# One set of state transfers for two batches, and a new instruction order, in a fused mLSTM and gated feed-forward kernel

## The chip, the cores and the metric

The kernel runs on one core of a Trainium2 chip. The metric is the device time of one execution in microseconds (us), as the median of several runs; less is better.

## The reference

The first half is an mLSTM with exponential gates over four batches, eight heads, 768 steps and a head width D of 40. The second half is a gated feed-forward network over the 3072 rows that come out of it.

```python
for t in range(S):                                   # S = 768
    m_new = np.maximum(f_gate[:, :, t] + m, i_gate[:, :, t])
    f_stab = np.exp(f_gate[:, :, t] + m - m_new)
    i_stab = np.exp(i_gate[:, :, t] - m_new)
    C = f_stab * C + i_stab * (v_t outer k_t)        # state, D x D for each head
    n = f_stab * n + i_stab * k_t
    y[:, :, t] = sigmoid(o_t) * (C q_t) / max(|n q_t|, 1)
x = y as (batch * step, head * D)                    # 3072 x 320
out = (sigmoid(x @ w_gate) * (x @ w_val)) @ w_out    # inner width 1536
```

## The kernel before

The steps are cut into six chunks of 128, so there are 24 units of work (chunk c, batch b), numbered u = 4c + b. Within a chunk the mLSTM is computed as masked attention: scores of q and k (`b` steps, line 778 for the first eight units and 783 from unit 8 on), times a decay matrix, times v (`c` steps, line 761). What the earlier chunks left behind enters through the state: the `ci` step (line 804) multiplies q by the state of its batch, and the `c` steps of chunks 1 to 4 also form the outer products of k and v that update the state (line 629).

The state lives in two forms. The tile `cst` holds the state of each head, two heads above each other, and is updated in place by VectorE, GpSimd or ScalarE (`z`, `zm` for chunk 0, `zd` and `za` later). The tile `cb` is a block-diagonal copy that `ci` reads as its right operand, three heads to a block. Since a block moves data to other partitions, it is filled by transfers: the `zs` steps, four for each unit of chunks 0 to 4, which the table `MOVES` lists (`moved`, line 923). That is 80 transfers.

From unit 8 on q and k are turned by a detour through memory: a step `a` transposes in blocks, `as` steps save pieces to the scratch tensors `scr0q`, `scr0k`, `scr1q`, `scr1k` (line 713, even and odd batches), `s` steps load them again as `qs` and `ks` (line 748), and `aq` steps load `qk` for `ci` (line 720). `ks` and `qs` have one buffer each, so the loads of a unit start when the scores of the unit before it are done.

The feed-forward half is 103 tiles of TensorE work: `t` steps are the up products (line 951, output 256 or 512 columns wide), `p` steps the down products (line 989). All large operands are held as a high and a low part. In the opening the weights are decoded by ScalarE and VectorE from loads named `st`.

Nearly all transfers are issued from one queue, SyncE's (SP), in program order. Each waits until the eighth transfer before it has landed. The order of all instructions on all engines is written out by hand in the string `ORDER`: a word is the next step of that name. An engine takes its instructions strictly in that order.

Of the kernel before, what the change touches and what calls it, by code (L numbers as in the profile page):

```python
# [9 lines left out]
F32 = mybir.dt.float32  # L10
# [132 lines left out]
p9*2 p10 t11 p9 t12 cf5 t12 p9 t12*2 w20f t12 tg11 p10 p9 gs w21e zs2 t12 w23d w25a k1d w25b w24a lo8 t12 e6 t12*2
w25b p10 t12 / b5.2 gs*2 k1d w23f p10 w24b t12 bm5.2 k1d t12*3 th11 tl11 al8.0 w24b p10*2 cx4 w24b w24d w23e / a6.2
t12 lo7 zd5 as8.3 ta12 p10 w24e p10 t12 w26a ah6.2 d4 w27a dx4 zs2 c5 cs5 cv5 dy4 t13 cv5 tg12 p11 t13*3 p11 w25b w24f
e6m lq7 t13 w26b t13 a6.1 w26b p11 ah6.1 lv9 t13 w27b w26b za5 th12 t13*3 p11 ct5 p11 cg5 t13 p11 cv5 w25d t13 w25e
p11*2 p12 w26d p12 p11 lk7 t13 lv6 / ci6 tl12 t13 w26e cr5 p11 w27b t13 as8.1 p12*2 e7a p12 w27b p12*2 ta13 lq9 t13
p12 t14*6 tg13 cf6 t14*3 cx5 aq6.0 d5 t14 a7.2 lo6 w27d p11 ld8 as8.0 a9.1 t14*2 zs4*2 w27e t14 p11 bk6 ah7.2 / b6.0
t14*2 aq6.2 p12 t14 as8.2 dx5 dy5 p12 zs4 aq6.1 th13 bm6.0 p13 b6.1 ct7 w27f w28a b6.2 tl13 aq7.2 bm6.1 zd7 bm6.2 e7m
ta14 w28b p13*2 t15*2 zd6 tg14 t15 a7.1 w28b lq11 ah7.1 w28b c6 t15*3 p12 t15 e8 a7.0 w28d p12 aq7.1 t15 za6 w28e ld9  # L150
th14 t15*2 p13 tl14 p13 w29a t15*2 ah7.0 t15 p13 lv8 t15*2 ct6 lk8 w29b p13 lv7 cs6 w29b ah9.1 cv6 ta15 zs5 p13 t15
w29b cg6 / ci7 w29d p13*2 p14 al9.1 cv6 tg15 t16 p13 t16 cf7 t16 p13 t16 aq8 t16 zs4 t16 th15 p14 zs6 as9.7 p14 t16*2
as9.5 bk7 / b7.1 w29e p14 as9.4 t16 aq8 t16 lq12 t16 p15 bm7.1 a8.1 p15 t16 p14 tl15 t16 p14*2 ah8.1 al8.1 t16 as8.4
p15 oh0 a9.0 t16 as9.6 cv6 / b7.2 ta16 t16 tg16 p15 p14 p15 p14 t17*2 as8.6 t17*3 o0 t17 as8.7 p14 t17 p14 p15*2 cr6
p15 bm7.2 aq7.0 b7.0 t17*2 ah9.0 th16 aq8 t17 p14 t17 tl16 p15 bm7.0 t17*4 ta17 p15 c7 cs7 oh1 p16 zs5 t17 tg17 al9.0
p15*2 t18 cx6 d6 t18 th17 p16 as8.5 t18*2 e8a t18*4 tl17 t18*2 ld10 a11.0 p16 dx6 dy6 p16 v8 t18 p17 o1 t18*5 p17 p16
as9.0 e8m p17 s8 p16 ta18 s8 p17 t19*2 cv7 tg18 cg7 t19*3 s8 t19*2 e9a oh3 th18 t19 p18 s8 bk8 a10.0 zs5 p17*2 t19*5
cv7 tl18 t19*2 / ci8 cf8 ct8 ta19 t19 p18 tg19 p18*2 t20*4 th19 as9.2 t20*4 / b8.2 ah10.0 o3 tl19 t20 bm8.2 cv7 v9
al10.0 t20*6 ta20 t20 p19 cr7 tg20 p19 oh2 lk10 p19 p18 th20 p18 lq14 as9.1 t21*2 p19 t21*6 tl20 za7 t21*2 e10a t21*2
p20 t21*3 ta21 cx7 / b8.1 b8.0 bm8.1 t21 p19 t22*2 tg21 t22*6 lo10 th21 a10.1 p20*2 p21 bm8.0 p19 zs7 p20 t22*2 lo9  # L160
p21 t22*2 p20 as9.3 t22*4 d7 e9 tl21 c8 ta22 tg22 t23*2 zs6*2 t23 ah10.1 as10.0 ah11.0 t23 p20 t23 zd8 cs8 cv8 s9*2
t23*4 al10.1 t23*2 th22 t23*2 as10.2 t23 p21 t23 aq9 p22*2 t23 dx7 tl22 p21*2 ta23 p22 tg23 p21 t24 th23 e9m bk9 t24
cv8 dy7 cv8 aq9 t24*2 p22 t24*5 as10.5 al11.0 zs6 p22 p23 t24 as10.6 t24*2 p22 t24 zs7 zs5 t24*2 cg8 p23 tl23 aq9 ci9
t24 ta24 s9 p23 t25*2 tg24 s9 as10.3 t25 lv11 t25*5 th24 p23 t25*3 v11 t25 za8 t25*3 p23 t25 p23 p24*2 tl24 as10.1 p24
ta25 t26*2 p24 as10.4 cf9 tg25 t26*2 ct10 t26*6 v10 t26*3 p24 t26 cr8 th25 t26 p24 tl25 lv10 t26 / b9.1 ta26 b9.0 t27
tg26 p25*2 bm9.1 p25*2 as10.7 t27*6 zs7 t27*4 zd10 t27*2 th26 t27*3 p25 p26 tl26 p26 b9.2 ta27 tg27 t28*3 o2 lk11
# [91 lines left out]
t102*4 p100*6 p101*2 o20 p101 ta102 tg102 th102 p101*2 p102*2 tl102 p102 oh22 o22 p101 p102*3 oh23 o23  # L258
"""
GROUPS = ((0, 3), (3, 3), (6, 2))  # L260
PAIRS = ((0, 3, 6, 2), (1, 4, 7, 5))
MOVES = ((0, 0, 0, 0, 3), (1, 1, 0, 0, 3), (2, 0, 3, 0, 1), (2, 1, 3, 1, 2))


@with_exitstack
def mlstm_then_gated_ffn_kernel(
# [13 lines left out]
    nc = tc.nc  # L280
    B, H, S, D = q.shape
    P = 128
# [926 lines left out]
```

## Time and profile before

| what | us |
|---|---|
| median of 3 runs | 518.26 (517.64 to 519.38) |
| the profiled execution, its own time | 519.33 |
| its span, first to last instruction | 517.6 |
| TensorE (PE) busy in the span | 501.0 (97%) |
| VectorE (DVE) / ScalarE (ACT) / GpSimd (POOL) busy | 311.6 / 190.5 / 154.5 |
| bytes moved by DMA | 76.67 MB in 234782 packets |

The profiled execution is 1.7 us longer than its span, and 1.07 us longer than the median of the runs. The granted TensorE clock is full over the whole span up to the last output. In the views, SPq means SP's queue: a row there is a transfer being issued. Such a row shows its issue, not its data.

### The profile page before, as it was taken

To read this page: it belongs to the slowest core of one execution; us is meant where nothing else is said; L and a number is where in the kernel's file an instruction comes from. 1 tells how busy PE (TensorE), PEld (TensorE's weight loads), DVE (VectorE), ACT (ScalarE), POOL (GpSimd) and SP (SyncE) were. 2 spreads that over 40 slices of the span, in tenths; PEclk is the share of its full clock that TensorE was granted. 3 is DMA by queue.
4 is the path that set the end of the run, shared out by engine and by line. 5 is a ranking of instruction groups with operands and counts; after the bars stand their busy time and mean duration, and the time that the engine had idled before them with its cause. 6 is when DMAs were issued, how large, how long until landed. Compare 5 with 4: busy or idle time off the path is not lost.

```text
span 517.6 us, 13246 instructions
## 1 busy us (share of the span) xinstructions
PE 501.0 (97%) x5191; PEld 453.0 (88%) x5191; DVE 311.6 (60%) x738; ACT 190.5 (37%) x483; POOL 154.5 (30%) x207
## 2 busy tenths in 40 slices
PE   7899999999998999999999999999999999999997
PEld 6678887889898999998887888888888888999997
DVE  8898989886653675655656464786544234434222
ACT  5876675653333324324213133211331441222221
POOL 3654342445352222331212242403241320101011
PEclk9999999999999999999999999999999999999999
DMA  8988886867968888996788689798699752010001
GB/s 194 209 220 215 231 229 170 180 149 141 201 128 172 171 184 174 183 206 109 154 169 141 152 172 201 142 175 170 151 166 215 135 115 77 26 27 15 13 1 39
DMA packets 234782, 76.67 MB, mean 148 GB/s; under 512 B 214240, under 2 KB 222624, under 8 KB 234720
## 3 DMA queue, kind: packets, MB, share of 16 engines
q1 hardware_dynamic: 233632, 75.56, 68.1%
q8 instruction: 41, 0.67, 0.5%
q10 hardware_dynamic: 1088, 0.26, 0.3%
q14 instruction: 21, 0.17, 0.1%
HBM read 57.61 MB, written 17.14 MB: 144 GB/s over the span
## 4 chain that ended last, share of the span: by engine, by line
PE 71%; DMA 9%; DVE 7%; SPq 6%; ACT 3%; issue 3%; POOL 1%; ACTq 0%; DVEq 0%
PE pg L951 42%; PE po L989 20%; PE av L761 2%; SPq L923 2%; PE s L783 2%; DMA st<-in_moe_w_val_dram 2%; PE in L804 2%; DMA qs<-scr1q 2%; DMA st<-in_moe_w_gate_dram 1%; DMA qs<-scr0q 1%; SPq L713 1%; DMA out_dram<-ob 1%; PE xt L888 1%; SPq L748 1%; DVE dc L535 1%
## 5 line engine op out<-in xcount | busy, mean ns | idle before, releaser
L964 ACT ACTIVATE sg<-pg 128x256 f32<-128x256 f32 (+1 forms) x103 | 48.3, 469 | 238.1 <-PE pg L951 211.1
L967 DVE SCALAR_TENSOR_TENSOR sg<-sg,pg 128x256 f32<-128x256 f32 (+1 forms) x103 | 54.0, 524 | 114.9 <-ACT sg L964 88.8
L978 POOL TENSOR_TENSOR gl<-sg,gh 128x256 fp32r<-128x256 f32 (+1 forms) x51 | 50.1, 982 | 233.6 <-ACT gh L972 82.9
L951 PE MATMUL pg<-xh,wh 128*128 128x256 f32 (+1 forms) x412 | 110.1, 338 | 0.6 <-ACT sg L964 0.5
L951 PE MATMUL pg<-xl,wh 128*128 128x256 f32 (+1 forms) x412 | 109.2, 329 | 0.5 <-DVE xl L901 0.4
L951 PE MATMUL pg<-xh,wl 128*128 128x256 f32 (+1 forms) x412 | 107.7, 331 | 0.0
L989 PE MATMUL po<-ol,gh 128*128 128x320 f32 x288 | 87.4, 314 | 0.0
L989 PE MATMUL po<-oh,gh 128*128 128x320 f32 x288 | 87.1, 315 | 0.3 <-ACT ob L1005 0.3
L989 PE MATMUL po<-oh,gl 128*128 128x320 f32 x288 | 85.7, 312 | 0.0
L951 PEld LDWEIGHTS pg<-xl,wh 128*128 128x128 f32 x412 | 69.8, 188 | 5.7 <-DVE xl L901 0.9
L951 PEld LDWEIGHTS pg<-xh,wh 128*128 128x128 f32 x412 | 69.1, 189 | 6.5 <-ACT sg L964 1.0
L951 PEld LDWEIGHTS pg<-xh,wl 128*128 128x128 f32 x412 | 68.9, 188 | 5.6
L951 PE MATMUL pg<-xl,w 128*128 128x256 f32 (+1 forms) x206 | 61.9, 334 | 0.0
L989 PEld LDWEIGHTS po<-oh,gh 128*128 128x128 f32 x288 | 53.2, 188 | 4.6 <-ACT ob L1005 0.7
L989 PEld LDWEIGHTS po<-ol,gh 128*128 128x128 f32 x288 | 53.4, 188 | 3.6
L989 PEld LDWEIGHTS po<-oh,gl 128*128 128x128 f32 x288 | 53.4, 188 | 3.5 <-DVE gl L978 0.2
L951 PE MATMUL pg<-xh,w 128*128 128x256 f32 (+1 forms) x206 | 55.0, 330 | 0.0
L789 DVE TENSOR_TENSOR d<-s,d 128x384 f32<-128x384 f32 (+1 forms) x66 | 32.8, 507 | 29.5 <-PE s L783 26.9
L972 ACT ACTIVATE gh<-sg 128x256 fp32r<-128x256 f32 (+1 forms) x58 | 28.9, 498 | 40.2 <-DVE sg L967 27.3
L481 ACT ACTIVATE d<-d,at 128x128 f32<-128x128 f32 x136 | 42.9, 390 | 0.0
L951 PEld LDWEIGHTS pg<-xl,w 128*128 128x128 f32 x206 | 36.7, 188 | 2.2
L951 PEld LDWEIGHTS pg<-xh,w 128*128 128x128 f32 x206 | 34.8, 188 | 2.5
(151 smaller groups left out, 671.6 us busy)
## 6 DMA issues: line engine op xcount, KB each, us to landing
d<-mscr SPq DMA_DIRECT2D x22, 512.0 KB
k<-in_k_dram SPq DMA_DIRECT2D x24, 160.0 KB
v<-in_v_dram SPq DMA_DIRECT2D x24, 160.0 KB
o<-in_o_gate_dram SPq DMA_DIRECT2D x24, 160.0 KB
st_o<-in_moe_w_out_dram SPq DMA_DIRECT2D x12, 320.0 KB
scr0q<-qt SPq DMA_DIRECT2D x32, 120.0 KB
out_dram<-ob SPq DMA_DIRECT2D x24, 160.0 KB
scr1q<-qt SPq DMA_DIRECT2D x32, 120.0 KB
```

What stands on the lines that cost most here:

```text
L481: nc.scalar.activation(d[:, h, :], d[:, h, :], AF.Exp, bias=at[:, c, b * H + h : b * H + h + 1], scale=-1.0)
L761: nc.tensor.matmul(dst[xs], lhs[:, xs], rhs, start=True, stop=True)
L783: nc.tensor.matmul(ps[g][:, m, :], ks[: 3 * D, h0 + m, :], qs[: 3 * D, h0 + m, :], start=True, stop=True)
L789: nc.vector.tensor_tensor(x, ps[g][:, :nh, :], x, ALU.mult)
L804: nc.tensor.matmul(pi[:, h0 : h0 + nh, :], qk[u][:r, g, :], cb[:r, b, g, : nh * DA], start=True, stop=True)
L923: nc.sync.dma_start(cb[j * D : (j + 1) * D, b, g0:g1, j * DA : (j + 1) * DA], pair_state(b)[88 * e : 88 * e + D, p0 : p0 + g1 - g0, :])
L951: nc.tensor.matmul(pg[x], w[:, a, fs] if a < 2 else w[:, fs], y[c][:, a, n0:n1], start=first, stop=a == 2 and y is xl)
L964: nc.scalar.activation(sg[0], pg[0], AF.Tanh, scale=0.5)
L967: nc.vector.scalar_tensor_tensor(sg[0], sg[0], 1.0, pg[1], ALU.add, ALU.mult)
L972: nc.scalar.activation(gh[u][:, :nt], sg[0], AF.Copy)
L978: E('gl0' if c == 0 else 'gl', f'tl{n}').tensor_tensor(gl[u][:, :nt], sg[0], gh[u][:, :nt].bitcast(F32), ALU.subtract)
L989: nc.tensor.matmul(po[t], g[c, j, t0][:, (t - t0) * P : (t - t0 + 1) * P], o[:, j, :], start=j == 0 and first, stop=j == NF - 1 and last)
```

## The change

The tiles `cst` and `cb` are laid out anew, so that the two batches of a pair (0 and 1, 2 and 3) stand beside each other. A `zs` step now moves the part of both batches, and only the odd batch of a pair has such steps: 40 transfers in place of 80, each with twice the rows. A row stays 41 numbers long, 164 bytes. A set now waits for the states of both batches, and, since it overwrites what `ci` reads, for the `ci` of both. `GAP` is 0, so the scratch tensors and their loads stay as they were.

`ORDER` differs from its 21st word on, in the opening too. Its words are the same but for the 40 that go.

```diff
-v1 lk1 lq1 iy ig v0 ig im ia ir is ig im ih igs iac ih x2
+v1 lk1 lq1 iy ig ir x2 ig ...
...
-    cb = const.tile([P, B, 3, 3 * DA], F32, name="cb")
+    cb = const.tile([P, B // 2, 3, 2, 3 * DA], F32, name="cb")
...
-            cst[0] = two.tile([P, B, 4, DA], F32, tag="cst", name="cst", bufs=1)
-        return cst[0][:, b]
+            cst[0] = two.tile([P, B // 2, 4, 2, DA], F32, tag="cst", name="cst", bufs=1)
+        return cst[0][:, b // 2, :, b % 2]
...
-                nc.tensor.matmul(pi[:, h0 : h0 + nh, :], qk[u][:r, g, :], cb[:r, b, g, : nh * DA], start=True, stop=True)
+                nc.tensor.matmul(pi[:, h0 : h0 + nh, :], qk[u][:r, g, :], cb[:r, b // 2, g, b % 2, : nh * DA], start=True, stop=True)
...
         def moved(j, e, p0, g0, g1):
-            nc.sync.dma_start(cb[j * D : (j + 1) * D, b, g0:g1, j * DA : (j + 1) * DA],
-                              pair_state(b)[88 * e : 88 * e + D, p0 : p0 + g1 - g0, :])
+            nc.sync.dma_start(cb[j * D : (j + 1) * D, b // 2, g0:g1, :, j * DA : (j + 1) * DA],
+                              cst[0][88 * e : 88 * e + D, b // 2, p0 : p0 + g1 - g0])
...
-        for x in MOVES:
-            put(f"zs{n}", moved, *x)
+        if b % 2:
+            for x in MOVES:
+                put(f"zs{n}", moved, *x)
```

SP's queue in front of unit 9's `ci` (chunk 2, batch 1; the rows name the batch alone, `ks_1`, `qk_1`, `qs_1`). Before:

```order
L748 DMA ks_1_2443<-scr1k 40x1024
L713 DMA scr0q<-qt_2_2214 32x30x32
L720 DMA qk_1_2462<-scr1q 40x3x128 x2
L713 DMA scr0k<-kt_2_2345 32x20x32
L923 DMA cb<-cst 40x41
L713 DMA scr0k<-kt_2_2345 32x20x32
L923 DMA cb<-cst 40x3x41
L923 DMA cb<-cst 40x41
L720 DMA qk_1_2462<-scr1q 40x2x128
L748 DMA qs_1_2524<-scr1q 80x1024
```

And of the change:

```order
L746 DMA ks_1_2333<-scr1k 40x1024
L718 DMA qk_1_2426<-scr1q 40x3x128
L349 DMA k_2_2428<-in_k_dram 128x8x40
L746 DMA qs_1_2436<-scr1q 80x1024
L746 DMA qs_1_2436<-scr1q 40x1024
L349 DMA k_3_2453<-in_k_dram 128x8x40
L711 DMA scr0q<-qt_2_2118 32x30x32
L718 DMA qk_1_2426<-scr1q 40x3x128
L718 DMA qk_1_2426<-scr1q 40x2x128
```

Three state transfers stood among the loads of `qk_1` and `qs_1`; none stands there now, `qs_1` is ahead of the last two loads of `qk_1`, and two loads of raw k have come in.

SP's queue in the opening, behind its first six loads (`st_0` are pieces of the weights, `mscr` is the store of the running maximum that waits for VectorE). Before:

```order
L1179 DMA mscr_79<-m_97 32x128
L551 DMA st_0_172<-in_moe_w_gate_dram 64x512
L551 DMA st_0_172<-in_moe_w_val_dram 64x512
L351 DMA v_0_142<-in_v_dram 128x8x40
L351 DMA o_1_193<-in_o_gate_dram 128x8x40
L351 DMA o_0_211<-in_o_gate_dram 128x8x40
```

And of the change:

```order
L549 DMA st_0_145<-in_moe_w_gate_dram 64x512
L549 DMA st_0_145<-in_moe_w_val_dram 64x512
L349 DMA v_1_132<-in_v_dram 128x8x40
L1178 DMA mscr_79<-m_97 32x128
L349 DMA o_1_242<-in_o_gate_dram 128x8x40
L349 DMA qpad_89<-in_q_dram 128x8x40
L349 DMA v_0_236<-in_v_dram 128x8x40
```

The two weight pieces and `v_1` go ahead of the store; `v_0`, which the first attention product reads, has moved back by three issues.

ScalarE a little later in the opening, around the first activation of a feed-forward tile (`sg_0_0`; `dc_1` are decoding steps of loaded weights, 512 wide for the gate and then the value weights). Before:

```order
L526 ACTIVATE dc_1_483<-st_1_303 128x512
L526 ACTIVATE dc_1_486<-st_1_339 128x256
L668 ACTIVATE kq_2_439<-pt_0_2_477 120x512
L481 ACTIVATE d_2_299<-d_2_299,at 128x128 x4
L918 ACTIVATE cst<-cs_0_502 128x164
L526 ACTIVATE dc_1_536<-st_1_437 128x512
L964 ACTIVATE sg_0_0_542<-pg_0_0_0_489 128x256
```

And of the change:

```order
L524 ACTIVATE dc_1_467<-st_1_439 128x512
L666 ACTIVATE kq_2_430<-pt_0_2_462 120x512
L479 ACTIVATE d_2_348<-d_2_348,at 128x128 x4
L916 ACTIVATE cst<-cs_0_480 128x4x41
L562 ACTIVATE wh_101<-dc_1_467 128x2x256
L524 ACTIVATE dc_1_539<-st_1_520 128x256
L963 ACTIVATE sg_0_0_542<-pg_0_0_0_469 128x256
L666 ACTIVATE kq_2_430<-pt_0_2_544 80x384
L971 ACTIVATE gh_0_0_555<-sg_0_0_542 128x256
L524 ACTIVATE dc_1_571<-st_1_533 128x512
```

The decoding of the value weights stood ahead of `sg_0_0`; it now stands three instructions behind it.

## Rows read from the trace of the kernel before

**Rows 1.** Busy time of each engine by stretch; PE is the first column
```profile
0.00:48.00 48.00, 40.85 (x602) 33.64 (x603) 42.70 (x110) 32.69 (x88) 24.15 (x46) 1.00 0.88 210
48.00:128.00 80.00, 78.48 (x721) 67.28 (x721) 70.50 (x168) 48.07 (x129) 34.03 (x38) 1.00 0.77 185
128.00:160.00 32.00, 29.17 (x404) 28.35 (x403) 16.16 (x42) 10.00 (x26) 14.60 (x21) 1.00 0.80 167
...
282.00:460.00 178.00, 177.72 (x1640) 157.32 (x1627) 90.71 (x199) 45.45 (x104) 44.31 (x50) 1.00 0.69 143
```

**Rows 2.** PE's timeline: start, us, instruction, idle before and releaser in brackets
```profile
139.90 0.41 PE L783 MATMUL s<-qs,ks 120*128 120x128 f32 x2 [1.27 <-DMA qs<-scr0q]
156.71 0.87 PE L804 MATMUL in<-cb,qk 120*128 120x123 f32 x6 [1.56 <-DMA qs<-scr1q]
...
264.34 0.45 PE L783 MATMUL s<-qs,ks 120*128 120x128 f32 x3
...
274.98 0.41 PE L783 MATMUL s<-qs,ks 120*128 120x128 f32 x2 [1.16 <-DMA qs<-scr1q]
```

**Rows 3.** The chain of waits ahead of unit 8's scores and unit 9's `ci`
```profile
118.92 0.63 PE in L804 x6
...
128.93 3.76 DMA scr0k<-kt
...
134.12 5.64 DMA qs<-scr0q
...
150.38 1.08 SPq L923
...
154.59 0.51 SPq L720
```

**Rows 4.** The chain of waits ahead of unit 15's scores
```profile
246.24 0.39 SPq L351
...
250.27 0.79 SPq L923
...
259.49 0.73 SPq L923
...
265.50 0.33 SPq L748
...
266.63 8.00 DMA qs<-scr1q
...
280.99 0.33 PE xt L888 x3
```

**Rows 5.** State transfers: all 80 by source line, then two on SP's timeline
```profile
L923 SPq DMA_DIRECT2D cb<-cst x80: 724/798/3012, 32.6 to 422.0; - x80
...
118.66 0.82 SPq L923 DMA_DIRECT2D cb<-cst  x1
...
160.88 0.74 SPq L923 DMA_DIRECT2D cb<-cst  x1
```

**Rows 6.** What a feed-forward matmul takes in a dense stretch, chain of waits
```profile
391.43 3.94 PE pg L951 x16
395.36 1.03 PE po L989 x7
```

**Rows 7.** The opening on PE, ACT and SP's queue
```profile
9.60 0.59 SPq L351 DMA_DIRECT2D v<-in_v_dram  x1
...
15.89 0.82 PE L761 MATMUL av<-v,d 128*32 128x41 f32 x64
...
19.48 0.52 SPq L351 DMA_DIRECT2D k<-in_k_dram  x1
...
25.79 0.30 PE L646 MATMUL pt<-ident,k 128*120 128x128 f32 x1 [0.87 <-DMA k<-in_k_dram]
...
28.24 0.67 ACT L526 ACTIVATE dc<-st 128x512 f32<-128x512 f32 x1 [1.57 <-DMA st<-in_moe_w_val_dram]
...
29.23 0.50 PE L951 MATMUL pg<-xh,wh 128*128 128x256 f32 x2 [0.55 <-ACT sg L964]
```

More of the change, by code (lines that the diff above doesn't have):

```diff
@@ L254 @@
[L254 to L258 removed]
+w26f w25f w29f w28f w21f iw ip*2 it if ii lq0 lk0 ib x0 x1 v1 lk1 lq1 iy ig ir x2 ig im ia gc*2 ig ih ig ih lv1 is im
@@ new lines @@
+zs13 t54 ct15 cg15 cv15 lk18 p52 t54 za15 cv15 cr15 tl53 p53*2 cx15 t54 / d15 t54 dx15 as16.6 t54 dx14 t54 ta54 t54
+dy15 p52 dy14 p53*2 p52*2 tg54 p52 a18.0 p53*2 a18.1 p53 t55*2 zs13 aq16 lk17 th54 s16*2 t55 tl54 t55*3 p53 t55*7
+s16*2 t55 p54 al17.0 p54 lo16 p54 t55*2 ta55 oh8 p54*3 oh9 o8 aq16 p53*2 zd16 bk16 tg55 p54 a17.1 ah17.1 t56*3 lv16
+ct16 t56 th55 lv17 o9 ah18.0 t56 al18.0 t56*2 tl55 t56*4 p54 t56 p55*2 aq16 t56*2 as17.1 t56 ta56 v17 t56 p54 v18
+p54*3 tg56 ld18 zs15 as17.3 / b16.0 b16.2 bm16.2 as17.0 p55 as18.0 oh11 zs13 o11 p55 t57 v16 t57*2 al17.1 t57*4 th56
@@ new lines @@
+as20.5 t66*3 b19.2 ct20 cx18 b19.0 bm19.2 t66*2 v21 bm19.0 t66 as20.7 lk21 d18 dx18 lq23 c19 cs19 dy18 ct19 as20.4
+cv19 cg19 tl65 t66*2 p65 t66 cv19 p65 p64*2 t66*2 p65 t66 ta66 p65 p64 cv19 cr19 cx19 d19 dx19 t66 p65*5 al21.0 as21.3
+t67 as20.2 dy19 t67 as20.3 t67 lk22 t67*3 tg66 t67 e20 a21.1 t67 p64 th66 t67*6 p66 tl66 e20a t67 ta67 t67 ah21.1
+p66*4 s20 p65 p66 t68 tg67 t68*3 oh12 p65 p66 al21.1 th67 t68 o12 t68 p65 aq20 p66 as21.6 a22.1 t68*4 za19 t68*3 s20
+zs17 p66 oh14 as21.7 as21.4 p66 o14 p66 ah22.1 t68*3 tl67 ta68 oh13 zs17 p67*4 e20m p67*2 t69*2 tg68 t69 th68 t69
@@ L259 @@
+t102 p100*2 tg102 p100*3 p101*4 th102 p101*2 tl102 p102*4 oh22 p102*2 oh23 o22 o23
 """
 GROUPS = ((0, 3), (3, 3), (6, 2))
+GAP = 0
 PAIRS = ((0, 3, 6, 2), (1, 4, 7, 5))
@@ L323, in mlstm_then_gated_ffn_kernel @@
     mscr = [dram.tile([BH, L], F32, name=f"mscr{c}", tag=f"mscr{c}") for c in range(NCH)]
-    scr = [[dram.tile([3 - x, D, H, L], F32, name=f"scr{n}{'qk'[x]}", tag=f"scr{n}{x}") for x in range(2)] for n in range(2)]
+    scr = [[dram.tile([3 - x, D, H, L + GAP], F32, name=f"scr{n}{'qk'[x]}", tag=f"scr{n}{x}") for x in range(2)] for n in range(2)]
     qt, kt, vt, ot = {}, {}, {}, {}
@@ L746, in take @@
             rows = slice(i * D, i * D + 2 * D) if whole else slice((2 - 2 * i) * D, (3 - 2 * i) * D)
-            src = sc[x][: 2 if whole else 1].rearrange("i d h t -> (i d) (h t)")
-            nc.sync.dma_start(dst[x][rows].rearrange("p h t -> p (h t)").bitcast(F32), src)
+            src = sc[x][: 2 if whole else 1].rearrange("i d h t -> (i d) h t")[:, :, :L]
+            nc.sync.dma_start(dst[x][rows].bitcast(F32), src)
             sks[c, b] = dst.get(1), dst.get(0)
```

266 lines of the change are left out of this document (126 added, 140 removed).

## The prediction

> **What bounds the kernel now.** The first view to read is the table of busy time by stretch. TensorE (PE) is busy for 501.0 of 517.6 us, so the work itself can't give much: the change leaves every matmul in place, and what can move is the 16.6 us in which PE stands still. The table says where these are [rows 1]: 48.00 - 40.85 = 7.15 us in the opening, 1.52 from 48 to 128 us, 2.83 from 128 to 160, and only 0.28 in the 178 us from 282 to 460. So the second half of the program is full, and a shorter transfer there is worth nothing.
>
> The second view is PE's timeline with the idle time before each piece [rows 2]. Three waits of more than a microsecond stand behind the opening: 1.27 us before the first scores of unit 8, 1.56 before unit 9's `ci`, 1.16 before the first scores of unit 15, together 3.99. All three end on a transfer. (The second is put down to `qs`, which `ci` doesn't read; it reads `qk`, issued just ahead of it.)
>
> The third view is the chain of waits, which tells why these transfers were late. Ahead of unit 15 it runs from 246.24 to 265.50 us through SP's queue alone, one issue behind the other, and seven of them are state transfers, the first at 250.27 and the last at 259.49 [rows 4]. Ahead of unit 9's `ci` three more stand between the last pieces it waits for, the first with 1.08 us [rows 3]. So SP's queue is a resource that PE waits for, at these places and not elsewhere.
>
> **The change, part by part.** *Issue time.* A state transfer holds the queue for 0.80 us in the median of 80 [rows 5]. The two single rows are one of 120 data rows, 0.82 us, and one of 40, 0.74 [rows 5]: 80 rows more cost 0.08. A merged one of 240 rows should then take 0.94 and one of 80 rows 0.78. A set for two batches falls from 4 x 0.82 + 4 x 0.74 = 6.24 us to 2 x 0.94 + 2 x 0.78 = 3.44, and ten sets free 28 us of the queue. If the issue doubled with the rows, they would free nothing. I take 28, since both rows are the operation itself, but PE gains only where the queue ends in a wait.
>
> The Trainium skill speaks against it ("DMA: Bandwidth & Descriptors", Bandwidth, the rule under the measured table): transfers under 64 KB are dominated by their descriptors, and the merged ones, 38.4 and 12.8 KB, still are, with as many rows in all. By that rule the merge frees nothing of the queue, and of the sum below only the opening's 0.8 us would stay: 517.4 us. For the issue the trace does not agree, by the 0.08 us of the sentence before; for the time of the data no row here shows it.
>
> *Unit 8's scores, 1.27 us.* The chain is a last save of k at 128.93, 3.76 us until it lands, then the loads, of which `qs` takes 5.64 [rows 3]. Counted in the order, 10 up products of 256 columns, 4 down products and a transpose more than before now stand between that save and the scores. A 512-column product takes 3.94 / 16 = 0.246 us, so one of 256 about 0.123, and a down product 1.03 / 7 = 0.147 [rows 6]; with 0.33 for the transpose [rows 4] the save has 2.1 us more. Between the last load and the scores one `ci`, 0.63 us [rows 3], is missing. Bounds for the wait that stays: 0, and 1.27 + 0.63 = 1.9. I take 0.3, nearer the end at which the chain begins.
>
> *Unit 9's `ci`, 1.56 us.* The three state transfers are gone from its stretch of the queue. Before, nothing stood on PE between the place of the last `qk` load and `ci`, and from that load's issue to `ci` it was 156.71 - 154.59 = 2.1 us [rows 2, 3]. Now 13 products of 256 columns and 2 down products stand there, 1.9 us. Bounds 0 and 1.56 (two loads of k have come into the queue, and the second of them can wait for a buffer); I take 0.15.
>
> *Unit 15's scores, 1.16 us.* `ks` and `qs` have one buffer, so the reload starts when unit 14's last scores end, at 264.34 + 0.45 = 264.79. The first scores of 15 start at 274.98 [rows 2]: 10.19 us, 9.03 of them filled with PE work. In the new order this stretch has one 512-column product, one down product and one `ci` fewer and a transpose more: 9.03 - 0.246 - 0.147 - 0.63 + 0.33 = 8.3 us. If the reload took as long, the wait would grow to 1.9. But of the queue ahead of it five of seven state transfers are gone, so the saves and the large decay load that stood right ahead leave some 4 us earlier, and the 8.00 us of the last load [rows 4], in full DMA traffic, should shorten. Bounds 0 and 1.9; I take 0.5, which asks 1.4 us of the reload, a third of those 4.
>
> *A new tight place.* Unit 21's reload had 37 up products of 512 columns to hide behind, now 22, with 14 down products, one `ci` and one gather: against unit 15's 9.03 us two up and two down products more and one `ci` less, 9.2 us. With 10.19 for the reload that is a wait of 1.0; bounds 0 and 1.0, I take 0.3.
>
> The waits together: 0.3 + 0.15 + 0.5 + 0.3 = 1.25 in place of 3.99, a gain of 2.7 us.
>
> *The opening.* Only its order changes, and here VectorE (DVE), busy 42.70 of 48.00 us [rows 1], sets the pace with PE. Two waits lose their cause: 0.87 us for the fourth unit's k, which is now issued ahead of two weight pieces, and 0.55 for ScalarE, whose activation stood behind a decoding step that waited 1.57 us for the value weights [rows 7]. That is 1.4 us. One load is worse off: `v_0` goes out three issues later, 3 x 0.59 = 1.8 us. It had 15.89 - 9.60 = 6.3 us from issue to use; the k load of 25.79 needed as much, from 19.48 [rows 7]. So it is late by 1.8 us, or not at all if it lands within 4.5; I take 0.6. Net gain 0.8. Bounds: a gain of 2.6, half of DVE's idle 5.3, and a loss of 1.8.
>
> *At nothing:* the stretch from 48 to 128 us keeps its idle 1.52 (bounds 0.5 and 3, since its order is new too, with DVE busy 70.50 of 80); everything from 282 us on, where PE has work at hand throughout [rows 1]; and the wait of a merged set for the later batch. The tightest such place is the first: 12 products of 256 columns and 5 down products, 2.2 us, lie between the last transfer to `cb` and the first `ci`, where 4.0 lay before. If the data take the 3.76 us of a save [rows 3], that costs 1.6.
>
> **Sum.** 517.6 - 2.7 - 0.8 = 514.1 us of span. With 1.7 us around the span that is 515.8 for the profiled execution, and since this one was 1.07 above the median, 514.7 us.
>
> **The rivals.** *Hidden anyway:* what was late were data, not issues. For it: 5.64 and 8.00 us of the chains are landing [rows 3, 4], and bytes and rows are the same. Then only `ci` of unit 9 gains: 1.27 + 0.15 + 1.9 + 1.0 = 4.3 us of waits against 3.99, an opening without change, 518.5 us. Against it: 19 us of one chain are issues alone. The rule of the Trainium skill above points this way.
>
> *Slower, the reload of the one buffer:* if it takes 12 us in place of 10.19, unit 15 waits 3.7 and unit 21 2.8; with 0.3 and 0.15 that is 6.9 us, 2.9 more than before, 521.2 us with an unchanged opening. For it: both stretches have become short by the new order. Against it: it would have to take longer with an emptier queue. It decides from 11.3 us on.
>
> *More than forecast:* all waits go and DVE's idle time in the opening halves: 517.6 - 3.99 - 2.6 + 0.6 = 511.6 us.
>
> **How the numbers follow.** The forecast gets 0.50, more than it 0.10, hidden anyway 0.24, the reload 0.16. About 0.3% (1.55 us) is what a measurement of this kernel tells from no change: faster is below 516.7, slower above 519.8. Faster takes 0.46 of the forecast and the 0.10; the same takes 0.04 of it and 0.23 of the second case; slower the reload and 0.01. The range goes from 511 (all waits and half of DVE's idle time gone) to 520.5, where most of the last case is left out. The forecast's own range is 512.5 to 517.
>
> **What would show it.** Right: `cb` issues of 0.78 to 0.95 us, 40 of them; no wait above 0.5 us before unit 9's `ci` and unit 8's scores; less than 6.5 us of PE idle in the first 48. Wrong: `cb` issues near 1.6 us; waits for `qs` above 1.5 us before units 15 or 21; a wait for `v` before the first gather; or new waits of PE for DVE between 48 and 128 us, of which this working knows least.

## The result: 0.65% slower, and the profile after

The changed kernel takes 521.77 us (median of 4 runs, 521.62 to 522.51), the kernel before 518.62 in the same comparison. The ratio is 1.0065 with a 95% interval of 1.0044 to 1.0085: slower, where 514.7 us was forecast and 520.5 was the upper end. (Medians in this text count every run; the ratios leave out one slow run each of `open_old_rest_new`, 682.8 us, and `merge_old_late`, 546.89 us, which move these medians by less than 0.2 us.)

The stretches of [rows 1], in the execution of the changed kernel (span 520.2 us; PE is the first column, DVE the third, the clock the first number behind the brackets):

```profile
0.00:48.00 48.00, 39.25 (x555) 32.26 (x556) 39.89 (x103) 30.58 (x80) 23.54 (x44) 0.96 0.79 193
48.00:128.00 80.00, 75.72 (x724) 63.08 (x723) 74.90 (x162) 49.66 (x135) 34.32 (x40) 1.00 0.78 186
128.00:160.00 32.00, 31.40 (x415) 30.25 (x414) 19.56 (x50) 9.59 (x23) 13.76 (x19) 1.00 0.76 161
...
282.00:460.00 178.00, 177.68 (x1690) 157.03 (x1690) 93.82 (x205) 46.65 (x105) 45.68 (x53) 1.00 0.71 147
```

PE's idle time is 8.75 us in the opening (7.15 before), 4.28 from 48 to 128 us (1.52 before), 0.60 from 128 to 160 (2.83 before), and 0.32 in the 178 us up to 460 (0.28 before). From 128 to 282 us as a whole, a stretch of 154 us, it has fallen from 4.34 to 1.16. With 1.3 us more of busy PE (502.3 against 501.0), the account closes: 517.6 + 1.60 + 2.76 - 3.18 + 0.04 + 1.33 = 520.2. The three waits of [rows 2] are gone: PE's timeline has no wait for a transfer at all. The loss lies ahead of 128 us.

The issue of a state transfer, over all 40 (the row that answers to [rows 5]; minimum, median, maximum in ns):

```profile
L921 SPq DMA_DIRECT2D cb<-cst x40: 768/817/2151, 49.4 to 424.6; - x40
```

A transfer of twice the rows takes 0.82 us in place of 0.80: by the medians the queue spends 33 us on them, not 64.

The opening, which answers to [rows 7], on PE, then VectorE (the kernel before in a fence of its own), then SP's queue, and last what SP's queue waited for from 12 to 26 us:

```profile
17.88 0.31 PE L644 MATMUL pt<-ident,k 128*80 128x128 f32 x1 [2.87 <-DVE d L1109]
...
27.97 0.50 PE L950 MATMUL pg<-xh,wh 128*128 128x256 f32 x2
```

```profile
16.93 0.43 DVE L537 SCALAR_TENSOR_TENSOR dc<-st,dc 128x256 int32<-128x256 int32 x1
17.28 1.35 DVE L1109 TENSOR_TENSOR d<-s,d 128x384 f32<-128x384 f32 x3
```

```profile
11.74 0.55 DVE L1110 TENSOR_TENSOR d<-s,d 128x384 f32<-128x384 f32 x1
```

```profile
15.30 0.43 SPq L545 DMA_DIRECT2D st<-in_moe_w_gate_dram  x1
22.65 0.37 SPq L349 DMA_DIRECT2D k<-in_k_dram  x1
```

```profile
SPq L349 <- PE cs L627: 6.9, 1, 6.9
```

These rows show a chain. The first multiplication of scores by the decay matrix starts at 17.28 us on VectorE, behind the decoding of three weight tensors (11.74 us before, behind one). PE waits 2.87 us for it. The product `cs` of the second unit, which frees a buffer of k, comes late for that reason, and the load of k for the fourth unit, which needs the buffer, holds the queue for 6.9 us. It goes out at 22.65 us, where before it went out at 19.48 [rows 7]. PE doesn't wait for it all the same, so what PE loses by this chain is the wait for VectorE; no row shows a price of the late load. The clock falls as well:

```profile
16.00:20.00 4.00, 2.12 (x69) 1.58 (x69) 3.11 (x7) 1.73 (x5) 1.97 (x4) 0.89 0.90 271
20.00:24.00 4.00, 4.00 (x124) 3.44 (x117) 2.81 (x11) 2.17 (x6) 3.52 (x5) 0.69 0.17 58
24.00:28.00 4.00, 2.36 (x20) 1.80 (x18) 2.92 (x11) 3.00 (x9) 0.86 (x1) 1.00 0.84 161
```

These windows of the changed kernel show a granted clock of 0.69 from 20 to 24 us, so the lower level (1.2 GHz) for part of it; before, it was full there (1.00). The work that PE didn't do in its busy time is 2.12 x 0.11 + 4.00 x 0.31 = 1.5 us, near the 1.33 by which busy PE has grown.

### The profile page after: what moved, and what is told of

Same layout as the page of the kernel before. It is cut to its first block, busy times and chain, and to the rows that moved or that the text cites. A ratio compares the mean times of both kernels' runs of the same rounds, so it can differ in the third digit from the quotient of the medians.

```text
span 520.2 us, 13187 instructions
## 1 busy us (share of the span) xinstructions
PE 502.3 (97%) x5191; PEld 453.6 (87%) x5191; DVE 318.8 (61%) x738; ACT 191.1 (37%) x483; POOL 156.8 (30%) x207
## 4 chain that ended last, share of the span: by engine, by line
PE 82%; DVE 11%; issue 2%; ACT 1%; DMA 1%; POOL 1%; SPq 0%; DVEq 0%; POOLq 0%
PE pg L950 47%; PE po L988 23%; PE av L759 3%; PE s L781 2%; PE in L802 2%; DVE dc L537 1%; PE xt L886 1%; DVE gl L977 1%; PE s L776 1%; DVE dc L529 1%; PE av L627 1%; DMA st_o<-in_moe_w_out_dram 1%; DVE sg L966 1%; DVE xl L899 1%; DMA gin<-in_f_gate_dram 1%
## 5 line engine op out<-in xcount | busy, mean ns | idle before, releaser
L950 PE MATMUL pg<-xh,wh 128*128 128x256 f32 (+1 forms) x412 | 107.6, 333 | 1.0 <-ACT sg L963 0.6
L977 POOL TENSOR_TENSOR gl<-sg,gh 128x256 fp32r<-128x256 f32 (+1 forms) x51 | 48.8, 958 | 196.1 <-ACT gh L971 63.1
L988 PE MATMUL po<-oh,gl 128*128 128x320 f32 x288 | 88.0, 315 | 1.3 <-DVE gl L977 1.1
L950 PE MATMUL pg<-xh,w 128*128 128x256 f32 (+1 forms) x206 | 53.6, 330 | 0.0
L977 DVE TENSOR_TENSOR gl<-sg,gh 128x256 fp32r<-128x256 f32 (+1 forms) x52 | 32.2, 619 | 14.4 <-ACT gh L971 7.0
```

What stands on the lines that cost most here:

```text
L950: nc.tensor.matmul(pg[x], w[:, a, fs] if a < 2 else w[:, fs], y[c][:, a, n0:n1], start=first, stop=a == 2 and y is xl)
L977: E('gl0' if c == 0 else 'gl', f'tl{n}').tensor_tensor(gl[u][:, :nt], sg[0], gh[u][:, :nt].bitcast(F32), ALU.subtract)
L988: nc.tensor.matmul(po[t], g[c, j, t0][:, (t - t0) * P : (t - t0 + 1) * P], o[:, j, :], start=j == 0 and first, stop=j == NF - 1 and last)
```

## The experiments

Three things differ between the kernels: the merge, the order of the opening, and the order behind it. At the 290th step of `ORDER` (about 37 us) and the 1130th (about 131 us) the two orders have done almost the same steps, so that one can be cut and the other put on. The table gives each kernel's idle time of PE by stretch and its busy PE, worked out from the busy time by stretch of its profiled execution. A ratio is to the kernel before in the same comparison, whose median there lies between 518.07 and 519.22 us. Busy PE differs by up to 2 us among the kernels whose clock stays full (499.7 to 501.7), so what is read from it is good to about 1 us.

| kernel | median us | ratio, 95% interval | idle 0 to 48 | 48 to 128 | 128 to 282 | busy PE |
|---|---|---|---|---|---|---|
| before | 518.6 | 1 | 7.15 | 1.52 | 4.34 | 501.0 |
| changed | 521.77 | 1.0044 to 1.0085 | 8.75 | 4.28 | 1.16 | 502.3 |
| merge_old_order | 522.27 | 1.0041 to 1.0079 | 6.18 | 1.50 | 5.53 | 504.0 |
| open_old_rest_new | 518.49 | 0.9978 to 1.0006 | 7.10 | 4.25 | 1.15 | 500.9 |
| open_new_rest_old | 527.82 | 1.0129 to 1.0176 | 8.32 | 2.04 | 6.43 | 506.5 |
| unmerged_new_order | 523.32 | 1.0063 to 1.0099 | 8.57 | 4.23 | 1.24 | 503.5 |
| old_to_131_merged | 514.76 | 0.9900 to 0.9955 | 6.48 | 1.54 | 1.04 | 499.7 |
| old_to_131_single | 516.12 | 0.9919 to 0.9959 | 6.09 | 1.53 | 1.50 | 501.7 |
| merge_old_late | 521.00 | 1.0021 to 1.0067 | 6.16 | 1.54 | 4.89 | 502.6 |
| merge_old_mixed | 515.76 | 0.9911 to 0.9962 | 5.78 | 1.51 | 1.76 | 500.8 |
| multiply_first | 521.50 | 1.0034 to 1.0078 | 7.02 | 4.30 | 1.18 | 503.3 |
| multiply_first_fill | 522.10 | 1.0034 to 1.0078 | 9.37 | 4.05 | 1.42 | 503.9 |
| open_new_mid_old | 519.58 | 0.9995 to 1.0030 | 8.47 | 2.06 | 0.98 | 501.7 |
| fill_the_wait | 522.21 | 1.0056 to 1.0093 | 7.23 | 4.39 | 1.18 | 504.2 (2.4 of it the filler) |

### The parts apart: four kernels

**The merge alone**, in the order of before. The layout of the changed kernel, and in `ORDER` the steps of a merged set where those of the even batch stood, or behind the last step they need:

```diff
-... t51 as15.4 zs12 za13 t51 p50 ah16.1 ...
+... t51 as15.4 za13 zs13*4 t51 p50 ah16.1 ...
```

> This kernel has the 40 merged transfers and the instruction order of before; each merged set stands where the set of the even batch stood, or behind the last step it needs. Theory A (the merge itself removes the three waits for transfers between 128 and 282 us, and the new order of the opening is what costs): waits for transfers fall from 3.99 us to under 1, the opening and 48 to 128 us stay as before (idle near 7.15 and 1.52 us), so 518.6 - 3.2 = 515.4 us. Rival B (the new order removes those waits, the merge does not): the three waits stay near 4 us, 518.6 us. Rival C (merged sets cost by themselves, since a set waits for two batches): a new wait for the block-diagonal tile, over 519 us. Either way the issue of a merged transfer is read here: 0.78 to 0.95 us if the rows are cheap, near 1.6 if it doubles.

Measured: 522.27 us. The issue is cheap, and from 128 to 160 us idle time falls from 2.83 to 0.73. But PE, now earlier, waits 4.33 us at unit 15's scores, and half clock follows (PE's timeline, then the windows of this kernel):

```profile
275.72 0.66 PE L783 MATMUL s<-qs,ks 120*128 120x128 f32 x2 [4.33 <-DMA qs<-scr1q]
```

```profile
276.00:280.00 4.00, 4.00 (x14) 3.52 (x14) 2.23 (x5) 0.47 (x1) 0.00 (x0) 0.50 0.96 154
280.00:284.00 4.00, 4.00 (x20) 3.58 (x19) 1.34 (x4) 0.60 (x1) 0.00 (x0) 0.75 0.00 0
```

At clocks of 0.50 and 0.75 these 8 us do the work of 5: 3.0 us lost, as much as busy PE has grown (504.0 - 501.0). So theory A holds at unit 9 and in part at unit 8 (0.73 us are left, for nothing that the profile shows) and fails at unit 15. The time is that of rival C, but the wait is for `qs` and not for the block-diagonal tile.

**The old opening with the new rest**, merged:

```diff
 (ORDER at the cut, marked |)
-... bm3.1 tl1 w8a w8b t2*2 | w9a t2*3 w9b ta2 ...
+... tl1 cg2 lv3 bm3.1 t2 cr2 | w5f ld4 w9a t2*3 ...
```

> Merged transfers; the order of before up to the 290th step (about the first 37 us), the order of the changed kernel from there. Theory A: the opening's PE idle falls back from 8.75 to about 7.2 us, its half clock (1.33 us more of busy PE) is gone, and 48 to 128 us falls back from 4.28 to near 1.5 us of idle, since VectorE no longer carries work of the opening into it; 521.8 - 1.6 - 1.3 - 2.8 = 516.1 us. Rival D (the loss between 48 and 128 us is due to the new order there): idle near 4.3 us stays in that stretch, 521.8 - 2.9 = 518.9 us.

Measured: 518.49 us. The opening is as before, with full clock. The stretch from 48 to 128 us is not:

```profile
0.00:48.00 48.00, 40.90 (x604) 33.99 (x605) 42.10 (x109) 32.33 (x87) 24.52 (x46) 1.00 0.88 210
48.00:128.00 80.00, 75.75 (x695) 63.37 (x694) 73.50 (x159) 49.03 (x133) 35.21 (x41) 1.00 0.76 182
```

So rival D holds, and theory A falls in its second part: the loss from 48 to 128 us is made by the order there, and is not carried over from the opening.

**The new opening with the old rest**, merged: the same cut, the other way round.

> Merged transfers; the order of the changed kernel up to the 290th step, the order of before from there. Theory A: the opening's loss (1.6 us idle, 1.3 us of half clock) and what it carries into 48 to 128 us (2.8 us) stay, the waits for transfers stay gone: 521 to 522 us. Rival B (the waits go by the order of the rest, not by the merge): the loss of 5.7 us stays and the 4 us of waits come back, 524.5 us. Rival D (the loss in 48 to 128 us is due to the order there): 521.8 - 2.8 = 519 us.

Measured: 527.82 us, worse than any of the three. The idle time from 48 to 128 us is back at 2.04, as rival D says; but waits for transfers are back too, as rival B says (1.05 us at unit 8's scores, 1.69 at unit 9's `ci`, and 3.35 at unit 15's scores, as with the merged sets of the first kernel), and the clock falls twice in the opening (0.78 from 16 to 20 us, 0.57 from 28 to 32) and once behind unit 15 (0.52 from 284 to 288).

**Single transfers in the new order:**

```diff
 (before, with the ORDER of the change, and in it)
-zs1
+zs0 zs1
```

> The 80 single transfers of before in the order of the changed kernel; the set of the even batch stands beside that of the odd one. Theory A: the opening's loss stays (2.9 us) with what it carries on (2.8 us), and the waits for transfers between 128 and 282 us come back, 3 to 4 us: 524 to 525 us. Rival B: the waits stay away, since the order keeps the queue clear in front of them: 521.5 to 522 us.

Measured: 523.32 us, and no wait for a transfer in the stretch in question (154 us of it, PE first):

```profile
128.00:282.00 154.00, 152.76 (x1781) 144.42 (x1780) 91.80 (x226) 48.66 (x126) 44.59 (x60) 1.00 0.79 164
```

Idle 1.24 us, where the changed kernel has 1.16. Rival B is right: the new order alone takes the three waits away. With single transfers too, no state transfer stands between the loads of `ks_1` and the last one of `qk_1`. Of the 0.9 us by which the span is longer, 0.87 have arisen by 24 us, in the opening.

### The best of both orders

```diff
 (ORDER of the change, and with that of before up to the cut, marked |)
-... t18*2 tg17 t18 cv7 th17 | a11.0 t18*2 za6 p16 ...
+... as8.5 t18*2 e8a t18*2 | v8 zd8 cv7 p16 a10.0 ...
```

> Merged transfers; the order of before up to the 1130th step (about 131 us), the order of the changed kernel from there. The runs so far say that the new order loses ahead of 128 us (opening 3.1 us, 48 to 128 us 2.7 us of idle) and gains behind it (idle 4.34 to 1.16 us). Theory E (these parts are independent): opening near 7.1 us of idle, 48 to 128 near 1.5, behind 128 us 1 to 2: 518.7 - 2.5 = 516.2 us, faster than both kernels. Rival F (the later gain is paid for by the earlier loss, since VectorE does work ahead in 48 to 128 us that it otherwise has to do later): the new waits of PE for VectorE come behind 131 us and the time stays at 518.5 us.

> The same order with the 80 single transfers, the even batch's set beside the odd one's. It tells what the merge is worth where the order is the better one. If only the order took the waits away, the time is that of the merged kernel within 0.5 us; if the queue's 32 us matter, waits for transfers of 1 to 3 us come back between 131 and 282 us and it is slower by as much.

Measured: 514.76 us merged, 516.12 single, both faster than both kernels. Theory E holds: the gain stays without the loss, and the merged kernel is even 1.4 us below the 516.2 forecast. The merge is worth some 1.4 us here by the medians and 0.6 by the ratios; the intervals overlap, so that its size is not settled. In the traces the merged kernel is 0.43 us ahead at 20 us, where no state transfer has been issued, 0.98 at 130 us, and 2.19 at 253 us, so 1.2 us of it arise between. Waits of 1 to 3 us have not come back with the single transfers; one of 0.42 us has, before unit 8's scores:

```profile
141.17 0.41 PE L782 MATMUL s<-qs,ks 120*128 120x128 f32 x2 [0.42 <-DMA qs<-scr0q]
```

### Where a merged set stands

Two more placings of the sets in the order of before. The first takes the later of the two old places of each step, where that is allowed:

> Merged transfers in the order of before once more, but each merged set stands at the later one of the two places at which the single sets stood (where it may). The first kernel of this kind lost at unit 15's scores: a wait of 4.33 us and half clock behind it, with a set of four transfers, which waited 2.3 us for a state, issued right ahead of the saves that these scores need. Theory H (the place of that set is the cause): unit 15's wait falls to 1 us or less, no half clock, 515.5 to 517 us. Rival I (the reload of the one buffer is the cause, since PE arrives 2.4 us earlier and the reload does not): a wait of 3 us or more and half clock stay, 521 to 522 us.

Measured: 521.00 us. Unit 15 doesn't wait. But now two transfers of a set go out only 5.7 us ahead of unit 8's `ci`, from 133.88 us, and PE most likely waits for them. (The row puts the wait down to a save that `ci` doesn't read, issued right behind them, so this is argued from what `ci` reads.)

```profile
139.56 0.87 PE L803 MATMUL in<-cb,qk 120*128 120x123 f32 x6 [3.62 <-DMA scr1q<-qt]
```

Half clock follows here as well (0.62 from 140 to 144 us). So theory H holds for unit 15 and not for the time: the wait has moved. The second is the first kernel with one set moved:

```diff
-... as15.4 za13 zs13*4 t51 p50 ... tg52 p50*2 p51 lo15 ...
+... as15.4 za13 t51 p50 ... tg52 p50 zs13*4 p50 p51 lo15 ...
```

> Merged transfers in the order of before, a third placing: the sets stand where the first of these kernels had them, but the set of chunk 3's first pair, which stood right ahead of the saves for unit 15's scores, stands behind the loads for these scores. Theory H (the place of a merged set decides): unit 15's wait falls from 4.33 us to 1.5 or less and the clock stays full: 515 to 516.5 us, so that the merge by itself is a gain of about 3 us if its sets are placed well. Rival I (the reload of the one buffer does not come earlier, whatever stands ahead of it): a wait of 3 us or more and half clock, 520 us or more.

Measured: 515.76 us. The last loads for unit 15 are issued from 263.12 us, in place of 267.08, and its scores start without a wait; that of unit 8 stays (PE's timeline of this kernel):

```profile
139.36 0.41 PE L783 MATMUL s<-qs,ks 120*128 120x128 f32 x2 [1.42 <-DMA qs<-scr0q]
...
271.19 0.34 PE L783 MATMUL s<-qs,ks 120*128 120x128 f32 x2
```

In the first kernel unit 14's scores end at 261.99 us and the loads go out from 266.31, so it was the queue ahead of them, and not the buffer, that held them. Theory H: in the old order the merge by itself is a gain of 0.4 to 0.9%, and moving one set of four transfers makes the difference to a loss of 0.6%.

### The opening

The multiplications ahead of the decoding (`ti01`, `ti00`, `ti02` are the multiplications, `wvb`, `wgb`, `wrb` decoding steps). In this kernel the k of unit 0 is weighted by a decay column that has been multiplied already, so its state is another than the reference's:

```diff
-wvb wra sp10 ex10 g wgb g wgb sc00 ... mk01 mk00 wrb lo0 bk0 wrb*2 ti01 x4 ... ti00 mk10 wvd ti02
+mk01 mk00 ti01 wvb wra sp10 ex10 g wgb g sc00 ti00 ti02 wgb ... wrb lo0 bk0 wrb*2 x4 ... mk10 wvd
```

> The changed kernel, with the first three multiplications of the scores by the decay matrix (L1109, d<-s) moved ahead of five to six decoding instructions of weights on VectorE. Theory A2 (the opening loses because these multiplications stand behind decoding; PE's wait of 2.87 us, the half clock behind it and the k load that blocks the queue until 22.65 us are its consequences): the wait falls under 1 us, the clock stays full, the opening's idle falls from 8.75 to about 7 us and busy PE by 1.3 us: 521.8 - 3 = 518.8 us, with the queue free again before 20 us. Rival G (the opening is late for its loads): the wait moves to another place of the opening and the time stays at 521 to 522 us.

Measured: 521.50 us. The wait of 2.87 us is gone, and idle time is 7.02 us, as theory A2 says. The clock is not cured: it stays at the lower level from about 20 to 28 us, and busy PE is 1.0 us above the changed kernel's. From 10 us on no wait of PE ahead of it is longer than 0.8 us, but the window from 16 us on is loose (2.56 of 4.00 busy; before 3.50):

```profile
16.00:20.00 4.00, 2.56 (x109) 1.83 (x111) 3.27 (x7) 1.97 (x5) 3.75 (x5) 1.00 1.00 337
20.00:24.00 4.00, 2.77 (x71) 2.38 (x72) 3.76 (x12) 2.18 (x6) 3.26 (x5) 0.56 0.57 103
24.00:28.00 4.00, 3.91 (x21) 3.48 (x20) 2.81 (x8) 3.27 (x9) 0.87 (x1) 0.59 0.73 212
```

The same with the k weighted first (`bk0`), and with a group of filler products moved (`im`):

```diff
-mk01 mk00 ti01 ... lo0 bk0 wrb*2 ... c0 ie sc12 iq cv0*2 ... cx1 im d1 iq
+mk01 mk00 bk0 ti01 ... lo0 wrb*2 ... c0 ie sc12 iq im cv0*2 ... cx1 d1 iq
```

> The changed kernel with the first multiplications ahead of the decoding, as before, now with the weighting of k by the decay (which reads the decay matrix) ahead of them, so that everything is computed as in the reference; and the last group of filler products of the opening (pwarm3x, eight products) moved from behind the second gather to a place ahead of the state's outer products, where TensorE waited 0.79 us. The kernel without the filler had 7.02 us of idle in the opening in place of 8.75, but half clock from 20 to 28 us. Theory J (the clock falls behind the loose stretch from 16 to 24 us and takes what the shorter waits give): full clock with the filler there, 519 to 520 us. Rival K (the filler delays the chain, or the clock falls all the same): 521 us or more.

Measured: 522.10 us, rival K. The profiled execution is the longest of its seven (523.96 us) and has a wait of 3.24 us at 21 to 24 us for nothing that the profile shows, so its opening says little; the time says that moving the filler gave nothing.

Filler added to the changed kernel, inside the wait:

```diff
-ex11 mk11 tr12
+ex11 mk11 iz tr12        (iz: ten products of 128 columns into a free PSUM bank)
```

> The changed kernel with ten filler products of 128 columns more (their result is read by nobody), ahead of the first transpose behind TensorE's wait of 2.87 us at 15.0 to 17.9 us, so that they lie inside this wait and delay nothing. Theory J2 (the fall of the clock to half from 17 to 24 us comes of TensorE standing idle there): full clock through the opening, busy PE without the filler 1.3 us less, 520.4 us. Rival N (the clock falls all the same, or its fall costs nothing that the chain sees): 521.8 us as before.

Measured: 522.21 us, rival N, and the windows tell why:

```profile
16.00:20.00 4.00, 3.35 (x82) 2.56 (x81) 3.25 (x8) 1.76 (x5) 1.96 (x4) 1.00 0.91 303
20.00:24.00 4.00, 3.19 (x110) 2.72 (x110) 3.59 (x12) 2.40 (x6) 3.58 (x5) 1.00 0.41 70
28.00:32.00 4.00, 3.91 (x47) 3.39 (x48) 3.34 (x7) 3.17 (x9) 2.11 (x3) 0.58 0.96 236
```

With the wait filled the clock stays full to 24 us. But it falls at 28 us instead, behind the next loose stretch (24 to 28 us, 2.27 of 4.00 busy). The new opening is loose in more than one place, and here the remedy at one was followed by a fall at the next; in the changed kernel the same stretch, 2.36 of 4.00 busy, left the clock full.

Last, the new opening with the better rest:

> Merged transfers; the opening of the changed kernel (290 steps, about 37 us), then the order of before up to the 1130th step (about 131 us), then the order of the changed kernel. If the opening's price stays where it arises (idle and half clock in the first 48 us), this is the best kernel so far plus 3.1 us: 517.9 us, with 48 to 128 us at 1.5 to 2 us of idle. If the late opening pushes work into 48 to 128 us, idle there is 3 us or more and the time 519.5 us or more.

Measured: 519.58 us, a ratio of 1.0012 against 0.9927 for the same kernel with the old opening. The opening costs 4.4 us by these ratios: in the traces 2.0 of idle time in the first 48 us, 2.0 of busy PE, 0.5 behind them. So nearly all of its price arises where the opening is, as the first case says, but it is more than the 3.1 us assumed; 48 to 128 us stays at 2.06.

### What the order did from 48 to 128 us

VectorE is busy for 74.90 us there in the changed kernel and for 70.50 before [rows 1], with fewer instructions (162 against 168). The rows by shape from 48 to 128 us (sum in us, then the mean in ns), of the kernel with the new order there (open_old_rest_new), and of the one with the old (old_to_131_merged):

```profile
L537 DVE SCALAR_TENSOR_TENSOR dc<-st,dc 128x512 int32<-128x512 int32 x8 | 7.0, 881 | 0.1
...
L977 DVE TENSOR_TENSOR gl<-sg,gh 128x512 fp32r<-128x512 f32 x5 | 4.9, 981 | 0.0
L584 DVE TENSOR_TENSOR ol<-dc,oh 128x320 fp32r<-128x320 f32 x2 | 2.4, 1204 | 0.0
```

```profile
L538 DVE SCALAR_TENSOR_TENSOR dc<-st,dc 128x512 int32<-128x512 int32 x8 | 5.5, 684 | 0.0
...
L978 DVE TENSOR_TENSOR gl<-sg,gh 128x512 fp32r<-128x512 f32 x5 | 3.7, 732 | 0.0
L585 DVE TENSOR_TENSOR ol<-dc,oh 128x320 fp32r<-128x320 f32 x2 | 1.4, 692 | 0.6 <-ACT oh L563 0.5
```

These three, equally often, take 29 to 74% longer. They aren't the whole: of the shapes that both kernels have equally often there, some take longer by 7.8 us in all and others shorter by 3.6 (`dc<-dc` 128x512 int32 took 597 ns with the old order and 417 with the new). An instruction that takes longer, in the changed kernel, with what GpSimd did beside it and what PE waited for (VectorE, GpSimd, PE):

```profile
106.80 1.31 DVE L977 TENSOR_TENSOR gl<-sg,gh 128x512 fp32r<-128x512 f32 x1
```

```profile
106.69 0.87 POOL L671 TENSOR_TENSOR kq<-qc,rmask 120x384 f32<-120x384 f32 x1
107.52 1.18 POOL L762 TENSOR_TENSOR k<-k,d 128x320 f32<-128x320 f32 x1
```

```profile
108.16 0.42 PE L988 MATMUL po<-oh,gl 128*128 128x320 f32 x1 [0.80 <-DVE gl L977]
```

To test it by itself, GpSimd computes the same thing beside VectorE in the kernel before, far from this stretch:

```diff
+            if 60 <= n < 90 and e is nc.vector:
+                nc.gpsimd.tensor_tensor(twin[0][:, :nt], sg[0], gh[u][:, :nt].bitcast(F32), ALU.subtract)
```

> The kernel before, with one thing added: in the feed-forward tiles 60 to 89, where VectorE computes the low part gl<-sg,gh, GpSimd computes the same thing once more into a tile that nobody reads, so that the two run side by side. Theory L (in the new order the same VectorE instructions take longer because GpSimd works on two operands beside them): gl of 128x512 on VectorE, 0.68 to 0.69 us there in the kernel before, takes 1.2 to 1.4 us. Rival M (the instructions are longer for another cause, such as traffic of transfers): it stays at 0.68 to 0.75 us. The time of the whole kernel is not the point.

Measured, on VectorE and then on GpSimd:

```profile
334.95 1.80 DVE L979 TENSOR_TENSOR gl<-sg,gh 128x512 fp32r<-128x512 f32 x1
...
358.46 0.68 DVE L979 TENSOR_TENSOR gl<-sg,gh 128x512 fp32r<-128x512 f32 x1
368.46 0.69 DVE L979 TENSOR_TENSOR gl<-sg,gh 128x512 fp32r<-128x512 f32 x1
392.50 1.40 DVE L979 TENSOR_TENSOR gl<-sg,gh 128x512 fp32r<-128x512 f32 x1
```

```profile
334.92 1.28 POOL L983 TENSOR_TENSOR twin<-sg,gh 128x512 fp32r<-128x512 f32 x1 [5.43 <-DVE gh L974]
...
368.50 1.81 POOL L983 TENSOR_TENSOR twin<-sg,gh 128x512 fp32r<-128x512 f32 x1 [6.00 <-DVE gh L974]
392.05 1.29 POOL L983 TENSOR_TENSOR twin<-sg,gh 128x512 fp32r<-128x512 f32 x1 [3.47 <-DVE gh L974]
```

Whichever starts second ends late. At 334.95 VectorE starts 0.03 us behind GpSimd and ends 0.55 us behind GpSimd's end (336.20); at 392.50 it ends 0.56 behind it (393.34). At 368.46 VectorE is first, takes 0.69, and GpSimd takes 1.81. Alone (358.46) it takes 0.68. Theory L holds: one waits until the other is through. This agrees with the Trainium skill ("SBUF — State Buffer", Who interferes with whom), which says that a VectorE instruction with two inputs in SBUF and a GpSimd instruction that reads SBUF lock each other out, and that the order of issue decides who waits.

The same mark is on the changed kernel. Its `gl` of 106.80 us ends at 108.11, 0.55 behind the `kq` on GpSimd that had begun before it (107.56). Of the 161 VectorE instructions that start between 48 and 128 us, 21 take at least 1.5 times as long as the same instruction (operation, shape, tiles) at its quickest in the traces of before, changed, open_old_rest_new and old_to_131_merged. Each of the 21 starts while GpSimd is at work and ends 0.14 to 0.55 us behind the GpSimd instruction that it met; eight of them are `dc<-dc` steps, which read one tile. In the kernel before it is 12 of 167. What these take beyond the quickest is 12.9 us against 5.8. PE's three longest waits of the stretch, 0.95 us at 62.09, 0.80 at 108.16 and 0.84 at 125.90, stand behind such instructions, the last behind this one (VectorE, then PE):

```profile
123.64 1.37 DVE L584 TENSOR_TENSOR ol<-dc,oh 128x320 fp32r<-128x320 f32 x1
```

```profile
125.90 0.88 PE L776 MATMUL s<-kq 120*128 120x384 f32 x2 [0.84 <-DVE kq L671]
```

## Why the prediction was wrong

*The issue time* was right in the sum: 64 - 33 = 31 us of the queue freed where 28 were forecast. By size it was 0.825 us for 240 rows (0.94 forecast) and 0.815 for 80 (0.78 forecast). That the merge frees nothing of the queue was the prediction's inference from the rule of the Trainium skill that it weighed ("DMA: Bandwidth & Descriptors", Bandwidth). The row decides: 40 transfers hold the queue half as long as 80 with the same rows in all.

*The three waits* were right in size: a gain of 2.7 forecast, 3.2 found, with none left at the places that got 0.3 to 0.5 us, and none before unit 21. The cause was wrong at units 9 and 15, where it was sought in the merge (at unit 8 it was the order). The step "The three state transfers are gone from its stretch of the queue" put the gain down to the merge; with single transfers the new order has it as well (idle 1.24 us). By the ratios the merge alone gives 3.3 us (merge_old_mixed), the new order from 131 us alone 3.2 (old_to_131_single) and both together 3.8: either does most of it, and they don't add up. One row was misread besides: the chain ahead of unit 15 isn't "SP's queue alone", since 2.74 us of it are the landing of a save, so that 16.5 us and not 19 are issues:

```profile
262.64 2.74 DMA scr1k<-kt
```

*The opening* is the first step that failed: "Net gain 0.8. Bounds: a gain of 2.6, half of DVE's idle 5.3, and a loss of 1.8." It lost 1.60 us of idle time and 1.33 of clock, 2.9 together, outside these bounds. Its three terms don't hold the loss: the two waits that it takes away are gone, and PE doesn't wait for `v_0`. What it has no term for is PE's wait of 2.87 us for VectorE's multiplication, and the clock. Two readings led there. "the fourth unit's k, which is now issued ahead of two weight pieces" read a place in a queue as a time: the load waits for a buffer, whose release had become later, and it went out 3.2 us later than before. And, which is the step that cost the time, VectorE's queue was not followed: the multiplications that PE waits for stood behind the decoding of three weight tensors in place of one. The order would have shown that, as it showed the loads. Undoing the opening's order gives back the idle time and the clock, and 3.3 us by the medians (521.77 - 518.49), 3.8 by the ratios. Moving the multiplications ahead gives back the idle time alone (7.02); why the clock falls there all the same stays open.

*48 to 128 us* is the second: "keeps its idle 1.52 (bounds 0.5 and 3 ...)". It became 4.28. The text said of this stretch that it knew least of it, and named PE's waits for VectorE there as a sign of being wrong; the price was set by the old row all the same. The work on VectorE is nearly the same, but it lasts longer, since it meets GpSimd's. That the order makes this loss is shown by the cut at 37 us (4.25 with the old opening) and the one at 131 us (1.54). That the lock is what lengthens VectorE's work is shown, by the test and by the 21 instructions. That it makes all of PE's 2.76 us is not: no run keeps the new order there and takes GpSimd's work away, and VectorE's instructions are not the same in number (159 with the new order, 165 with the old).

*The sum* by its own terms: 514.1 forecast; the opening 0.8 + 1.6 + 1.3 = 3.7 worse, the middle 2.8 worse, the waits 0.5 better, which is 520.1, and the span was 520.2.

*The rivals.* The one for "slower" gave 521.2, near the result, by another mechanism: a reload of the one buffer that takes 12 us. In the changed kernel PE waits for no reload, so that the nearness is chance. With the merge in the old order unit 15 did wait, 4.33 us, but for loads that the queue held back and not for the buffer. *Hidden anyway* falls too: all three waits went.

## What to carry to other kernels

When an order is laid anew, follow each engine's queue to the first place where PE waits for it, the compute engines as well as the loads, and ask of each load that has moved up what frees its buffer. Price a stretch in which VectorE is busy for nine tenths by what runs on GpSimd beside it, since 21 instructions there took at least half as long again. And take a change of layout and a change of order apart before judging either: here the order of before up to 131 us, with the rest of the new order and the merge, is 0.7% faster than the kernel before.

## What the runs showed of the hardware

After PE's waits of 2.64 to 4.33 us, in seven of the kernels, the granted clock fell to the lower level for some us; behind unit 15's scores this cost 3.0 us on top of a wait of 4.33. The waits of 1.27 to 1.56 us of [rows 2] left it full. It also fell behind a stretch of 4 us with 2.56 busy and no wait above 0.8 us. How it decides is not settled by these runs: in the changed kernel a window with 2.36 of 4.00 busy (24 to 28 us) left it full, and with the wait filled one with 2.27 at the same place did not.

A VectorE instruction that starts beside a GpSimd one can take until 0.14 to 0.55 us behind that one's end (the 21 of the changed kernel): 1.31 us for a 128x512 subtraction that takes 0.68 alone. Steps that read one tile (`dc<-dc`) are hit as well as those that read two.
